# Nesting a width-wise two-output trick into two of six positions of a row-wise fast convolution, in a residual block

## The chip, the cores and the metric

The kernel runs on one core of one Trainium2 chip. The metric is the device time of one execution in microseconds (us).

Engines: PE is TensorE (PEld its weight loads), DVE is VectorE, ACT is ScalarE, POOL is GpSimd, SP issues most DMAs. "L565" is line 565 of the kernel that the line of the profile belongs to.

## The reference

```python
# B, C, H, W = 2, 512, 64, 64; everything in bfloat16
h = conv3(silu(gn(x, g1, be1)), w1)          # gn: group norm, 4 groups of 128 channels
h = h + (silu(t_emb) @ w_emb).reshape(B, C, 1, 1)   # t_emb: 2 x 1152
h = conv3(silu(gn(h, g2, be2)), w2)          # conv3: 3x3, zero padding, C to C channels
return x + h
```

## The kernel before

Both convolutions use a fast algorithm along the rows. Four output rows come from six "positions": the input rows are combined into six tensors V, the weights into six tensors U, each position is a convolution along the width only, and the six results are combined into four rows. A **set** is one block of 128 output channels for one chunk of 32 rows. It is 6 positions x 4 input blocks (of 128 channels) x 3 taps along the width = 72 matmuls of 512 columns. There are 4 output blocks x 4 chunks (2 images x 2) x 2 layers = 32 sets: 1 to 16 are layer 1, 17 to 32 layer 2, four sets to a chunk.

The six accumulators of a set (in PSUM) are evacuated four by ScalarE and two by VectorE:

```python
    stage = ctx.enter_context(tc.tile_pool(name="stage", bufs=4))     # weights as they arrive
    ps_acc = ctx.enter_context(tc.tile_pool(name="ps_acc", bufs=6, space=PSUM))
    POS_ORDER = (1, 2, 3, 4, 0, 5)
    ...
                def mm(pos, ct, kx, first, last):
                    nc.tensor.matmul(                                                 # L565
                        accs[pos][:], lhsT=U[ct][:, SLOT[pos], kx, :], rhs=V[:, ct, SLOT[pos], :, kx:kx + W],
                        start=first, stop=last)
    ...
                def evac(pos):
                    if pos in (1, 2, 3, 4):
                        ...
                        i_a = nc.scalar.activation(out=msl[:, SLOT[pos]], in_=accs[pos][:], ...)   # L579
                    if pos == 4:
                        nc.vector.tensor_tensor(out=sts[:, 0:2], in0=msl[:, 0:2], in1=msl[:, 2:4], op=ALU.subtract)
                        ... # seven more, and in layer 2 three that add x (the residual)
                    elif pos in (0, 5):
                        nc.vector.scalar_tensor_tensor(out=y4[:, (0, 3)[k]], in0=accs[pos][:], ...)   # L599
                    if pos == 5:
                        ... # layer 1: square for the second norm, store to h_scr; layer 2: store to out
```

Everything else (weights' preparation `prep_U`, the input tensors `produce_V`, the statistics of the norms, the embedding) is cut into small steps that a scheduler mixes into the sets ahead of a deadline. In the traces each engine takes its instructions in the order of the program.

Of the kernel before, what the change touches and what calls it, by code (L numbers as in the profile page):

```python
# [64 lines left out]
def kernel(  # L65
# [33 lines left out]
    N_SUM_ACT = 1  # L99
    assert C % P == 0 and E % P == 0 and C // 4 == P and H % CR == 0 and NFREE == 512  # L100
# [8 lines left out]
    stage = ctx.enter_context(tc.tile_pool(name="stage", bufs=4))  # L109
    wtmp = ctx.enter_context(tc.tile_pool(name="wtmp", bufs=2))  # L110
    vpool = ctx.enter_context(tc.tile_pool(name="V", bufs=2))
    srcp = ctx.enter_context(tc.tile_pool(name="src", bufs=2))
    otmp = ctx.enter_context(tc.tile_pool(name="otmp", bufs=1))
    stg = ctx.enter_context(tc.tile_pool(name="stg", bufs=2))
    small = ctx.enter_context(tc.tile_pool(name="small", bufs=4))
# [21 lines left out]
    k_tmp = [consts.tile([P, 2, TR, TH, WP], F16, name=f"k_tmp{i}") for i in range(2)]  # L137
    x_tmp = consts.tile([P, TR, 2, WP], F16, name="x_tmp")
    sum_w = consts.tile([P, NCH, 5], F32, name="sum_w")
    for i, wgt in enumerate((1.0, 1.0, 2.0, 6.0, 2.0)):  # L140
        nc.vector.memset(sum_w[:, :, i:i + 1], wgt)
# [52 lines left out]
    def gram_pe(pieces, pool, tag):  # L194
        gr = pool.tile([P, NFREE], F32, tag=tag, name="gr")
        grf = gr[:, 0:P]
        blocks = [pc[:, j * P:(j + 1) * P] for pc in pieces for j in range(pc.shape[1] // P)]
        for j, blk in enumerate(blocks):
            nc.tensor.matmul(grf, lhsT=blk, rhs=blk, start=(j == 0), stop=(j == len(blocks) - 1))
        return grf  # L200

    def colsum_pe(pieces, pool, tag):
        cs = pool.tile([P, NFREE], F32, tag=tag, name="cs")
        blocks = [pc[:, k * NFREE:(k + 1) * NFREE] for pc in pieces for k in range(pc.shape[1] // NFREE)]
        for k, blk in enumerate(blocks):
            nc.tensor.matmul(cs[:], lhsT=ones_bf[:], rhs=blk, start=(k == 0), stop=(k == len(blocks) - 1))
# [26 lines left out]
    def me_colsum(me_col, cs):  # L233
        junk0 = wtmp.tile([P, NFREE], BF16, tag="sc")
        nc.scalar.activation(out=junk0[:], in_=cs[:], func=ACT.Identity,
# [4 lines left out]
    def gn1_stats_bg(b, ct, dep=None):  # L240
        hp = HW // 2
        pieces = []
        for k in range(2):
            xt = stg.tile([P, hp], BF16, tag="xr")
# [46 lines left out]
    def prep_U(layer, ot, ct, eng=None, dep=None):  # L291
# [3 lines left out]
        U = upool.tile([P, NPOS, NKX, P], F16, tag="U")  # L295
        Ut[layer][ot][ct] = U
# [14 lines left out]
        sc = wtmp.tile([P, 2, NKX, P], F16, tag="scp")  # L311
        nc.vector.tensor_scalar(out=sc[:, 0], in0=g0, scalar1=0.25, scalar2=None, op0=ALU.mult)
        nc.vector.tensor_scalar(out=gg[:, 0], in0=gg[:, 1], scalar1=0.5, scalar2=None, op0=ALU.mult)
        nc.vector.tensor_tensor(out=sc[:, 1], in0=g0, in1=g2, op=ALU.add)  # L314
        nc.vector.tensor_tensor(out=sc[:, 0], in0=sc[:, 0], in1=g2, op=ALU.add)  # L315
        yield
        nc.vector.tensor_tensor(out=U[:, 0:2], in0=sc[:], in1=gg[:], op=ALU.add)  # L317
        nc.vector.tensor_tensor(out=U[:, 2:4], in0=sc[:], in1=gg[:], op=ALU.subtract)  # L318
        yield

# [28 lines left out]
    POS_ORDER = (1, 2, 3, 4, 0, 5)  # L349
    SLOT = {3: 0, 1: 1, 4: 2, 2: 3, 0: 4, 5: 5}  # L350
    Vt = {}
    V_STEPS = 3 * CT

    def produce_V(layer, b, ch, resident=None, V=None):
        if V is None:
            V = vpool.tile([P, CT, NPOS, TR, WP], F16, tag="V")
        Vt[(layer, b, ch)] = V
        r0 = ch * CR - 1
        lo, hi = max(r0, 0), min(r0 + CR + 2, H)
        for ct in range(CT):  # L360
            at = a_tmp[ct % 2]
            if ch == 0:
                nc.gpsimd.memset(at[:, 0, 1:W + 1], 0.0)
            if ch == NCH - 1:
                nc.gpsimd.memset(at[:, CR + 1, 1:W + 1], 0.0)
            if resident is None:
                src = srcp.tile([P, CR + 2, W], BF16 if layer == 0 else F16, tag="src")
                src_dram = x_v[b, ct] if layer == 0 else h_scr[b, ct]
                nc.sync.dma_start(
                    out=src[:, lo - r0:hi - r0, :],  # L370
                    in_=src_dram[:, lo * W:hi * W].rearrange("p (r w) -> p r w", w=W),
                )
                srcs = [(lo, hi, src[:, lo - r0:hi - r0, :])]
            else:
                srcs = []
                for (rs, re, ap3) in resident[ct]:
                    a_, b_ = max(lo, rs), min(hi, re)
                    if a_ < b_:
                        srcs.append((a_, b_, ap3[:, a_ - rs:b_ - rs, :]))
            for (a_, b_, ap) in srcs:  # L380
                nc.scalar.activation(  # L381
                    out=at[:, a_ - r0:b_ - r0, 1:W + 1], in_=ap,
                    func=ACT.Silu, bias=nb_all[:, layer, b, ct:ct + 1],
                    scale=sc_all[:, layer, b, ct:ct + 1],
                )
            kt = k_tmp[ct % 2]

            def rows2(j):
                return at[:, j:j + CR, :].rearrange("p (t f) w -> p t (f w)", f=TH)[:, :, 0:2 * WP]

            nc.scalar.activation(out=kt[:, 1, :, 1:3].rearrange("p t f w -> p t (f w)"), in_=rows2(1),  # L391
                                 func=ACT.Copy, scale=4.0)
            yield
            nc.vector.tensor_tensor(  # L394
                out=kt[:, 0].rearrange("p t f w -> p (t f w)"),
# [42 lines left out]
    for ct in range(CT):  # L438
# [15 lines left out]
        if ct == 0:  # L454
            for g in gens_U0[1:]:
                next(g)
# [209 lines left out]
```

## Time and profile before

| | before |
|---|---|
| time, median of 15 runs | 564.81 us (563.0 to 565.33) |
| profiled span, clock | 563.3 us, 0.995 |
| PE / DVE / ACT busy | 543.4 / 372.5 / 278.2 us |
| an undisturbed set (72 matmuls) | 15.70 us |
| first matmul of set 1; end of the last matmul | 27.3 us; 558.5 us |

From the page of the kernel before: the busy times (first line), then the rows of the busy tenths in 40 equal slices of 14 us.

```profile
PE 543.4 (96%) x2814; PEld 260.8 (46%) x2814; DVE 372.5 (66%) x983; ACT 278.2 (49%) x380; POOL 22.5 (4%) x74
...
PE   5889999999999999999999989999999999999996
...
DVE  2889997489848732994659989399445942223444
ACT  5779999978825732565437348145212211111110
...
PEclk9999999999999999999999999999999999999999
```

TensorE is the limit nearly everywhere. VectorE and ScalarE are nearly full for several slices near the start, and VectorE again in slices 17 and 18 and from 22 to 25. The groups of instructions of the kernel before (line, engine, operation, output and inputs, shapes, count, then busy us, mean ns of one, idle time before it and what ended it):

```profile
L565 PE MATMUL acc<-V,U 128*128 128x512 f16 x2304 | 511.8, 382 | 0.9 <-DVE V L405 0.6
...
L579 ACT ACTIVATE msl<-acc 128x512 f16<-128x512 f32 x128 | 75.8, 593 | 176.2 <-PE acc L565 174.6
...
L599 DVE SCALAR_TENSOR_TENSOR yst<-acc,tt 128x512 f16<-128x512 f32 (+1 forms) x64 | 42.3, 681 | 3.6 <-PE acc L565 3.6
```

A matmul's own 382 ns is its pipelined length; what counts is the distance from one start to the next, which the trace shows as 216 ns in the median (mostly 215 to 223, 218 on average). 72 x 218 ns = 15.70 us a set. TensorE waited only 0.9 us in all in front of these 2304 matmuls.

### The profile page before, as it was taken

How to read it: one execution, taken by the hardware profiler on the slowest of the kernel's cores; microseconds unless marked ns; L12 is line 12 of the kernel's file. 1: busy time of each engine (PE TensorE's matmuls, PEld its weight loads, DVE VectorE, ACT ScalarE, POOL GpSimd, SP SyncE). 2: the span in 40 equal slices, each digit the busy share in tenths (PEclk: the TensorE clock that was granted, in tenths of full speed). 3: DMA queues.
4: the chain of work that ended last, by engine and by line, in shares of the span. 5: the costliest groups of instructions: out<-in, count | busy, mean ns of one | idle time of the engine just before them, and what ended most of it. 6: DMA issues, size and time to landing. Idle time of an engine off the chain costs nothing.

```text
span 563.3 us, 7506 instructions
## 1 busy us (share of the span) xinstructions
PE 543.4 (96%) x2814; PEld 260.8 (46%) x2814; DVE 372.5 (66%) x983; ACT 278.2 (49%) x380; POOL 22.5 (4%) x74
## 2 busy tenths in 40 slices
PE   5889999999999999999999989999999999999996
PEld 4645544444444444444455545444444444444442
DVE  2889997489848732994659989399445942223444
ACT  5779999978825732565437348145212211111110
POOL 1110000111002000000000020000000000000000
PEclk9999999999999999999999999999999999999999
DMA  8517453445701320033223324324221022222200
GB/s 334 211 40 247 157 165 134 143 153 137 261 11 68 106 86 37 39 114 110 70 80 104 135 67 146 113 76 151 76 74 54 24 74 75 76 74 76 74 38 37
DMA packets 18752, 59.81 MB, mean 106 GB/s; under 512 B 2075, under 2 KB 3227, under 8 KB 18331
## 3 DMA queue, kind: packets, MB, share of 16 engines
q1 hardware_dynamic: 18656, 59.32, 31.7%
q8 instruction: 22, 0.36, 0.3%
q14 instruction: 15, 0.12, 0.1%
q10 hardware_dynamic: 59, 0.01, 0.0%
HBM read 42.54 MB, written 16.78 MB: 105 GB/s over the span
## 4 chain that ended last, share of the span: by engine, by line
PE 67%; DVE 22%; ACT 5%; DMA 2%; issue 1%; POOL 1%; DVEq 0%; SPq 0%; ACTq 0%
PE acc L565 65%; DVE U L317 2%; DVE U L318 2%; DVE k_tmp L394 2%; ACT xt L216 2%; DVE yst L599 1%; ACT xt L212 1%; DVE V L408 1%; DVE V L406 1%; DVE V L405 1%; DVE sc L315 1%; DVE sc L314 1%; DVE k_tmp L399 1%; DMA xbuf<-in_x_dram 1%; ACT msl L579 1%
## 5 line engine op out<-in xcount | busy, mean ns | idle before, releaser
L565 PE MATMUL acc<-V,U 128*128 128x512 f16 x2304 | 511.8, 382 | 0.9 <-DVE V L405 0.6
L565 PEld LDWEIGHTS <-U 128*128 128x128 f16 x2304 | 224.3, 98 | 269.5 <-issue 3.3
L579 ACT ACTIVATE msl<-acc 128x512 f16<-128x512 f32 x128 | 75.8, 593 | 176.2 <-PE acc L565 174.6
L584 DVE TENSOR_TENSOR sts<-msl 128x1024 f16<-128x1024 f16 x32 | 22.0, 688 | 138.5 <-ACT msl L579 138.4
L381 ACT ACTIVATE a_tmp<-src,nb_all,sc_all 128x2112 f16<-128x2112 f16 (+1 forms) x28 | 60.2, 2154 | 23.8 <-DVE nb_all L279 5.9
L606 ACT ACTIVATE junk<-yst 128x2048 f16<-128x2048 f16 x16 | 30.6, 1910 | 33.4 <-DVE yst L599 33.2
L599 DVE SCALAR_TENSOR_TENSOR yst<-acc,tt 128x512 f16<-128x512 f32 (+1 forms) x64 | 42.3, 681 | 3.6 <-PE acc L565 3.6
L391 ACT ACTIVATE k_tmp<-a_tmp 128x1056 f16<-128x1056 f16 x32 | 34.7, 1086 | 16.1 <-DVE V L406 15.9
L394 DVE TENSOR_TENSOR k_tmp<-a_tmp 128x2112 f16<-128x2112 f16 x32 | 40.0, 1249 | 2.5 <-ACT a_tmp L381 2.4
L306 ACT ACTIVATE U<-pa 128x768 f16<-128x768 bf16 x32 | 26.3, 821 | 16.5 <-PE pa L302 16.2
L399 DVE TENSOR_TENSOR k_tmp<-k_tmp,a_tmp 128x1056 f16<-128x1056 f16 x32 | 22.4, 700 | 0.0
L405 DVE TENSOR_TENSOR V<-k_tmp 128x1056 f16<-128x1056 f16 x32 | 22.4, 699 | 0.0
L406 DVE TENSOR_TENSOR V<-k_tmp 128x1056 f16<-128x1056 f16 x32 | 22.4, 699 | 0.0
L408 DVE TENSOR_TENSOR V<-k_tmp,x_tmp 128x1056 f16<-128x1056 f16 x32 | 22.4, 699 | 0.0
L585 DVE TENSOR_TENSOR sts<-msl 128x1024 f16<-128x1024 f16 x32 | 21.8, 683 | 0.0
L302 PEld LDWEIGHTS <-wn 128*128 128x128 bf16 x192 | 16.9, 144 | 10.1 <-issue 5.2
L302 PE MATMUL pa<-ident,wn 128*128 128x128 bf16 x192 | 17.4, 229 | 4.0 <-DVE tot L165 2.8
L317 DVE TENSOR_TENSOR U<-sc,gg 128x768 f16<-128x768 f16 x32 | 17.5, 548 | 0.3
L318 DVE TENSOR_TENSOR U<-sc,gg 128x768 f16<-128x768 f16 x32 | 17.5, 546 | 0.0
L308 ACT ACTIVATE gg<-pb 128x384 f16<-128x384 bf16 x32 | 16.1, 503 | 0.1
L216 ACT ACTIVATE xt<-xt 128x2048 bf16<-128x2048 bf16 x8 | 15.3, 1918 | 0.0
L212 ACT ACTIVATE xt<-xt 128x2048 bf16<-128x2048 bf16 x8 | 15.3, 1918 | 0.0
(83 smaller groups left out, 308.7 us busy)
## 6 DMA issues: line engine op xcount, KB each, us to landing
wn<-in_w_dram SPq DMA_DIRECT2D x32, 288.0 KB, 3.3
src<-h_scr SPq DMA_DIRECT2D x16, 528.0 KB, 3.8
h_scr<-yst SPq DMA_DIRECT2D x16, 512.0 KB, 2.9
xr<-in_x_dram SPq DMA_DIRECT2D x16, 512.0 KB, 4.1
out_dram<-yst SPq DMA_DIRECT2D x16, 512.0 KB, 3.7
src<-in_x_dram SPq DMA_DIRECT2D x12, 528.0 KB, 3.9
xt<-in_x_dram SPq DMA_DIRECT2D x8, 512.0 KB, 4.9
xbuf<-in_x_dram SPq DMA_DIRECT2D x3, 1024.0 KB, 6.3
```

Of the source, the lines that this page charges most:

```text
L302: nc.tensor.transpose(pa[:, j, kx, :], wn_v[:, 2 * j, kx, :], ident[:])
L317: nc.vector.tensor_tensor(out=U[:, 0:2], in0=sc[:], in1=gg[:], op=ALU.add)
L318: nc.vector.tensor_tensor(out=U[:, 2:4], in0=sc[:], in1=gg[:], op=ALU.subtract)
L381: nc.scalar.activation(out=at[:, a_ - r0:b_ - r0, 1:W + 1], in_=ap, func=ACT.Silu, bias=nb_all[:, layer, b, ct:ct + 1], scale=sc_all[:, la ...
L391: nc.scalar.activation(out=kt[:, 1, :, 1:3].rearrange("p t f w -> p t (f w)"), in_=rows2(1), func=ACT.Copy, scale=4.0)
L394: nc.vector.tensor_tensor(out=kt[:, 0].rearrange("p t f w -> p (t f w)"), in0=at[:, 2:CR + 2].rearrange("p r w -> p (r w)"), in1=at[:, 0:C ...
L399: nc.vector.tensor_tensor(out=pq, in0=pq, in1=rows2(3), op=ALU.subtract)
L405: nc.vector.tensor_tensor(out=Vc[:, 0:2], in0=rp, in1=sq, op=ALU.add)
L565: nc.tensor.matmul(accs[pos][:], lhsT=U[ct][:, SLOT[pos], kx, :], rhs=V[:, ct, SLOT[pos], :, kx:kx + W], start=first, stop=last)
L579: i_a = nc.scalar.activation(out=msl[:, SLOT[pos]], in_=accs[pos][:], func=ACT.Copy if not kw else ACT.Identity, scale=KAPPA, **kw)
L599: nc.vector.scalar_tensor_tensor(out=y4[:, (0, 3)[k]], in0=accs[pos][:], scalar=(0.25 / WS, 1.0 / WS)[k], in1=tt[:, k], op0=ALU.mult, op1= ...
L606: nc.scalar.activation(out=junk[:], in_=yf, func=ACT.Square, scale=float(HW) ** -0.5, accum_out=ssq[:, ch:ch + 1])
```

## The change

The intent is to do less on the engine that is the limit. Take two neighbouring output columns of one position, with inputs d0..d3 and taps U0, U1, U2:

```
even = U0 d0 + U1 d1 + U2 d2  =  U0 d0 + U1 (d1 + d2)  -  (U1 - U2) d2
odd  = U0 d1 + U1 d2 + U2 d3  =  U0 d1 + U2 (d2 + d3)  +  (U1 - U2) d2
```

The last product is shared. If the sums S = d + (d shifted by one) and Ud = U1 - U2 are at hand, one block costs one matmul of 512 columns and three of 256, 1280 columns in place of 1536. The change does this for two of the six positions (3 and 4), in 28 of the 32 sets (not in the first chunk of layer 1). The matmuls then read every second column. The core of the diff:

```diff
-        accs[pos][:], lhsT=U[ct][:, SLOT[pos], kx, :], rhs=V[:, ct, SLOT[pos], :, kx:kx + W], ...
+    if pos not in nsl:            # plain positions: as before                         (L597)
+    ...
+    S = Vc[:, NPOS + i]
+    nc.tensor.matmul(acc[:], lhsT=Uc[:, s_, 0], rhs=Vc[:, s_, :, 0:W].rearrange("p t (j h) -> p h t j", h=2), ...)   # L604
+    nc.tensor.matmul(acc[:, 0:NH]..., lhsT=Uc[:, s_, 1], rhs=S[:, :, 1:W:2], ...)              # L606
+    nc.tensor.matmul(acc[:, NH:2 * NH]..., lhsT=Uc[:, s_, 2], rhs=S[:, :, 2:W + 1:2], ...)     # L608
+    nc.tensor.matmul(accs["w"][:, i * NH:(i + 1) * NH], lhsT=Ud[:, i], rhs=Vc[:, s_, :, 2:W + 1:2], ...)  # L610
```

The rest makes room for it or follows from it (cuts are marked by "..."):

```diff
# evictions: all six positions on ScalarE, the nested ones written with step two; accumulator w twice
-  nc.vector.scalar_tensor_tensor(out=y4[:, (0, 3)[k]], in0=accs[pos][:], ..., in1=tt[:, k], ...)
+  nc.scalar.activation(out=y4[:, 3 * k], in_=accs[pos][:]..., ...)                               # L617
+  if pos in nsl: dst = dst.rearrange("p (n h) -> p h n", h=2)
+  nc.scalar.activation(out=dst, in_=accs[pos][:]..., scale=KAPPA, ...)                           # L625
+  for h in range(2):
+      nc.scalar.activation(out=wv[:, h], in_=accs["w"][:], scale=(-KAPPA, KAPPA)[h], ...)        # L632
# VectorE adds w (L638), combines (L639-L646), adds into the outer rows at the end (L658)
# nested sums, one per V tile, and Ud, one per U tile
+  nc.vector.tensor_tensor(out=vf[:, NPOS:NSL, 0:n - 1], in0=vf[:, 0:NEST + 1:2, 0:n - 1],
+                          in1=vf[:, 0:NEST + 1:2, 1:n], op=ALU.add)                              # L425
+  nc.vector.tensor_tensor(out=Ud, in0=U[:, 0:3:2, 1], in1=U[:, 0:3:2, 2], op=ALU.subtract)
# memory: V is one tile per input block (8 slots for 6), one k_tmp, fewer staging buffers
-  stage = tile_pool(name="stage", bufs=4)
+  stage = tile_pool(name="stage", bufs=3)
# residual of layer 2: x is copied to out by DMA early, the results are added to it by DMA (not in the last set)
+  nc.sync.dma_start(out=out_v[b, ct][:, cs_], in_=x_v[b, ct][:, cs_])                            # 16 copies
-  nc.sync.dma_start(out=out_v[b, ot][:, rows], in_=flat(yst))
+  nc.gpsimd.dma_start(out=out_v[b, ot][:, rows], in_=flat(yst), accum_op=ALU.add)
# first loads: with three staging buffers, weights 2 and 3 of set 1 are loaded after all of x
-  for g in gens_U0[1:]: next(g)      # directly after x block 0
+  for g in gens_U0[1:2]: next(g)     # weight 1 only; 2 and 3 come after x blocks 1 to 3
```

## The prediction

> **What bounds the kernel now.** TensorE. The page of the profile has it busy 543.4 of 563.3 us at a granted clock of 0.995; 2304 matmuls of 512 columns make 32 sets (4 output blocks x 4 row chunks x 2 layers) of 72. In the chain of waits twelve in a row take 2.62 us, 218 ns each, so 15.7 us a set. Counting matmuls in windows of the trace, sets 9-14 and 20-31 run at 15.6-15.9 us. The others lose: the start (first conv matmul at 27.3 us), sets 2-3 (19.1, 17.9 us), sets 15-19 (16.7, 17.2, 18.3, 18.7, 22.5 us), where layer 2's weights are prepared. In the windows VectorE and ScalarE are 100% busy at 40-80 us, VectorE at 300-320 us.
>
> **What the change does.** In 28 of 32 sets (not the first chunk of layer 1) two of six positions replace three 512-column matmuls per input block by one of 512 and three of 256. In the trace 32 back-to-back 128-column matmuls with their weight loads took 1.79 us (56 ns each); between 56 and 218 ns I estimate 110 ns for 256 columns. Saved: 2x218-3x110 = 106 ns, x8 = 0.85 us a set, 23.8 us in all. The moving reads step by two elements; the Trainium skill (SBUF — State Buffer, the note on cachelines) says accesses within one 16-byte line keep full bandwidth, which step two does. No run shows it yet.
>
> Per set, durations from the instruction groups less about 0.08 us overlap: ScalarE evacuates all six positions plus the shared accumulator twice, four more evictions of 0.59 us. VectorE drops two of 0.68 us and, in layer 2, the residual adds (1.3 us), which become accumulating DMAs; it gains a 1024-element add (0.6). V costs VectorE 5.2-5.9 us per input block instead of 4.2; its nested sum reads one operand off by one element, without 4-byte alignment, so I take the single rate, 1.2 us (VectorE: DVE Perf Modes, mode 2x_1P). Sums over the instruction order: VectorE 372 to about 391 us, ScalarE 278 to about 345 us.
>
> **How much lands.** Sets 9-16, 20-32: TensorE stays the limit, 0.85 x 21 = 17.8 us gained. Sets 17-19: VectorE's work is 57 us before and after, against 50 us of TensorE; they took 59.5 and gain nothing. Sets 1-8: ScalarE has 69 us for sets 3-6 against TensorE's 63, VectorE 51 instead of 41 us in sets 2-4, and 16 copies of x to the output enter the DMA queue ahead of weights: the 3.4 us due there are lost again. The tail, now eviction, add, store: +0.8 us. ScalarE and VectorE wait for each other twice a set; I allow 2.5 us. 564 - 17.8 + 0.8 + 2.5 = 549.5 us.
>
> **Prediction: 549.5 us, 541 to 560 (8 in 10). Faster by over 2%: 0.62; within 2%: 0.32; slower: 0.06.**
>
> **What would show it.** 256-column matmuls about 110 ns apart; late sets at 14.9 us; ScalarE near 345 us; the nested sum at 1.2 us; sets 17-19 still 18-20 us each; set 8 ending at 163-169 us (166 now); TensorE idle for ScalarE's evictions in sets 3-7.
>
> **What would make it wrong.** Strided reads at half rate (over 100 us lost, late sets 19 us or more); weight loads not hidden behind 256 columns; the copies delaying sets 2-3 by more than a few us; ScalarE late enough to fill the six accumulators; accumulating DMAs that hold output buffers or lengthen the tail.

## More of the kernel before

The embedding, `emb_task`, loads nine weight pieces through the `stage` buffers that the convolution's weights use too, makes a silu on ScalarE and 36 small matmuls:

```python
        nc.scalar.activation(out=s_sb[...], in_=ps_t[:], func=ACT.Silu)          # L329
        yield
        for i in range(EMB_NP):                                                  # 5 loads, of up to two pieces
            wt = stage.tile([P, EMB_PIECE, C], BF16, tag="stage")
            nc.sync.dma_start(out=wt[:, 0:n, :], in_=wemb_v[:, e0:e0 + n, :])
            ps_e = ps_x.tile([P, CT, B], F32, tag="x")
            ... matmul(ps_e, lhsT=wt, rhs=s_sb)                                  # L339
            ... emb_sb += ps_e                                                   # VectorE
            yield
```

## The result and the profile after

| | before | after |
|---|---|---|
| time, median (range), runs | 564.81 (563.0 to 565.33), 15 | 559.17 (557.37 to 560.29), 10 |
| ratio of fast runs, 95% interval | | 0.9903 (0.9889 to 0.9917) |
| profiled span, clock | 563.3 us, 0.995 | 557.2 us, 0.985 |
| an undisturbed set | 15.70 us | 15.13 us |
| first matmul of set 1; end of the last | 27.3; 558.5 us | 29.1; 550.3 us |

A ratio is the mean time of one kernel's fast runs over that of the other's fast runs of the same rounds, so it is not quite the ratio of the medians. The change is a gain of 1%, within the 2% that counts as the same. The time lies inside the predicted range of 541 to 560 us, but the gain is 5.6 us where 14.5 were predicted, and "within 2%" had been given a chance of 0.32.

The page of the kernel after, the same rows:

```profile
PE 530.7 (95%) x3038; PEld 282.1 (51%) x3038; DVE 386.2 (69%) x1025; ACT 355.1 (64%) x531; POOL 36.3 (7%) x89
...
PE   5789999999799999999999989999999999999995
...
DVE  3589999833899895497569999779534972223334
ACT  4458679999767485798669855578435833332332
...
PEclk9989999999799999999999999999999999999999
```

TensorE has 12.7 us less work, of which 6.1 us of span came. The slice from 139 to 153 us (the eleventh) is new: PE and PEclk both fall to 7. The groups that answer to those of before, and the new ones:

```profile
L597 PE MATMUL acc<-V,Uf 128*128 128x512 f16 x1632 | 368.2, 383 | 5.5 <-DVE V L416 5.5
...
L625 ACT ACTIVATE ms<-acc 128x512 f16<-128x512 f32 x128 | 83.8, 660 | 85.5 <-PE acc L608 43.0
...
L604 PE MATMUL acc<-V,Uf 128*128 128x512 f16 x224 | 89.1, 398 | 0.0
...
L617 ACT ACTIVATE yst<-acc 128x512 f16<-128x512 f32 (+1 forms) x64 | 38.6, 603 | 47.4 <-PE acc L597 36.8
...
L632 ACT ACTIVATE yst<-accw 128x512 f16<-128x512 f32 x56 | 37.5, 744 | 0.0
```

ScalarE's plain eviction takes 603 ns, the ones that write with step two 744 ns (L632). The 660 of L625 mixes both kinds: in the trace 72 plain ones took 592 ns and 56 with step two 748. The nested sum and, for comparison, a VectorE instruction of nearly the same size whose operands are all aligned, from the groups of VectorE (the first row of the whole run, the second of 28 to 190 us):

```profile
L425 DVE TENSOR_TENSOR V<-V 128x1054 f16<-128x1054 f16 x28 | 19.7, 704 | 0.1
L416 DVE TENSOR_TENSOR V<-V 128x1056 f16<-128x1056 f16 x13 | 9.1, 699 | 0.0
```

A stretch of a late set of the kernel after, from the timeline (start us, length us, engine, line, operation):

```profile
436.13 0.39 PE L604 MATMUL acc<-V,Uf 128*128 128x512 f16 x1
436.36 0.28 PE L606 MATMUL acc<-V,Uf 128*128 128x256 f16 x1
436.48 0.28 PE L608 MATMUL acc<-V,Uf 128*128 128x256 f16 x1
436.59 0.28 PE L610 MATMUL accw<-V,Uf 128*128 128x256 f16 x1
436.71 0.39 PE L604 MATMUL acc<-V,Uf 128*128 128x512 f16 x1
```

From 436.13 to 436.71 one nested block takes 0.58 us. Over sets 25 to 32 the median distances to the next start are 233, 116, 116 and 118 ns, 583 together, where three plain matmuls take 3 x 218 = 654.

**Where the time went, by sets.** The table is worked out from the starts of the convolution's matmuls in the two traces (us; a set's length is the distance to the next set's start).

```
                      before    after    gain
start of set 1         27.35    29.09   -1.74
set 1                  20.07    22.80   -2.73
sets 2-6 (sum)         87.51    83.06   +4.45
set 7                  16.32    22.23   -5.91
set 8                  15.70    15.13   +0.57
sets 9-16 (sum)       129.41   124.96   +4.44
sets 17-19 (sum)       57.90    56.24   +1.65
sets 20-32 (sum)      204.26   196.81   +7.45
after the last matmul   4.78     6.86   -2.08
span                  563.29   557.18   +6.12
```

Three places give back what the sets gain: the start with set 1 (4.5 us), set 7 (5.9 us) and the tail (2.1 us). Set 7 is where the embedding's small products stand in TensorE's queue. From the timeline of TensorE, set 7 before:

```profile
134.50 0.56 PE L339 MATMUL ps_e<-s_sb,wt 128*128 128x2 bf16 x16 [1.02 <-ACT s_sb L329]
134.93 2.78 PE L565 MATMUL acc<-V,U 128*128 128x512 f16 x12
```

and after:

```profile
146.08 0.56 PE L355 MATMUL ps_e<-s_sb,wt 128*128 128x2 bf16 x16 [3.28 <-ACT s_sb L345]
...
148.42 0.63 PE L604 MATMUL acc<-V,Uf 128*128 128x512 f16 x1
148.84 0.41 PE L606 MATMUL acc<-V,Uf 128*128 128x256 f16 x1
149.06 0.41 PE L608 MATMUL acc<-V,Uf 128*128 128x256 f16 x1
149.27 0.41 PE L610 MATMUL accw<-V,Uf 128*128 128x256 f16 x1
149.48 0.63 PE L604 MATMUL acc<-V,Uf 128*128 128x512 f16 x1
...
151.62 1.48 PE L597 MATMUL acc<-V,Uf 128*128 128x512 f16 x6
```

A wait of 1.02 us for the silu became one of 3.28 us, and for the next five microseconds the matmuls of 256 and 512 columns stand 213 and 426 ns apart, twice the usual distance of a plain matmul. The Trainium skill (TensorE: Matmul & The Clock Gate, Part 1) says that TensorE's clock is halved after an idle window of about 3.4 us and gives 426.7 ns for 512 columns at half clock, 215.7 at full. The trace agrees with the two distances, 426 and 216 ns, and the half clock here follows a wait of 3.28 us. (In the kernel before, plain matmuls at half clock, from 336 to 339 us, stand 425 to 428 ns apart, no less than the strided ones here: the extra cost of strided reads, described below, does not show at half clock.) So the set pays twice: 3.3 us of waiting, and half of about 5.1 us at half clock, some 2.6 us more.

The tail, from the timeline: before,

```profile
557.71 0.68 DVE L595 TENSOR_TENSOR yst<-qs,xr 128x1024 bf16<-128x1024 f16 x1
558.31 1.28 DVE L599 SCALAR_TENSOR_TENSOR yst<-acc,tt 128x512 bf16<-128x512 f32 x2
559.62 0.33 SPq L610 DMA_DIRECT2D out_dram<-yst  x1
```

and after:

```profile
550.36 0.60 ACT L617 ACTIVATE yst<-acc 128x512 bf16<-128x512 f32 x1 [2.01 <-PE acc L597]
...
551.27 0.68 DVE L649 TENSOR_TENSOR yst<-yst,xr 128x1024 bf16<-128x1024 bf16 x1
551.88 0.68 DVE L648 TENSOR_TENSOR ms<-ms,xr 128x1024 f16<-128x1024 f16 x1
552.66 0.69 DVE L658 TENSOR_TENSOR yst<-yst,ms 128x1024 bf16<-128x1024 bf16 x1
553.38 0.34 SPq L665 DMA_DIRECT2D out_dram<-yst  x1
```

The last eviction is done at 550.96, but VectorE is still combining the nested positions until 552.6, and the final add starts 1.7 us after the eviction. Before, VectorE took the last accumulator itself and added in the same instruction.

### The profile page after: what moved, and what is told of

Read it like the earlier page. It is cut to its first block, busy times and chain, and to the rows that moved or that the text cites. A ratio compares the mean times of both kernels' runs of the same rounds, so it can differ in the third digit from the quotient of the medians.

```text
span 557.2 us, 8149 instructions
## 1 busy us (share of the span) xinstructions
PE 530.7 (95%) x3038; PEld 282.1 (51%) x3038; DVE 386.2 (69%) x1025; ACT 355.1 (64%) x531; POOL 36.3 (7%) x89
## 4 chain that ended last, share of the span: by engine, by line
PE 65%; DVE 24%; ACT 6%; DMA 2%; POOL 1%; issue 1%; SPq 0%; DVEq 0%; ACTq 0%
PE acc L597 43%; PE acc L604 8%; PE acc L606 4%; PE acc L608 4%; PE accw L610 4%; DVE Uf L323 2%; DVE Uf L322 2%; DVE V L416 1%; DVE V L412 1%; DVE V L411 1%; ACT xt L221 1%; DMA wn<-in_w_dram 1%; DVE k_tmp L413 1%; DVE V L417 1%; PE gr L204 1%; ACT xt L217 1%
## 5 line engine op out<-in xcount | busy, mean ns | idle before, releaser
L597 PE MATMUL acc<-V,Uf 128*128 128x512 f16 x1632 | 368.2, 383 | 5.5 <-DVE V L416 5.5
L597 PEld LDWEIGHTS <-Uf 128*128 128x128 f16 x1632 | 159.6, 99 | 191.7 <-issue 9.7
L625 ACT ACTIVATE ms<-acc 128x512 f16<-128x512 f32 x128 | 83.8, 660 | 85.5 <-PE acc L608 43.0
L604 PE MATMUL acc<-V,Uf 128*128 128x512 f16 x224 | 89.1, 398 | 0.0
L617 ACT ACTIVATE yst<-acc 128x512 f16<-128x512 f32 (+1 forms) x64 | 38.6, 603 | 47.4 <-PE acc L597 36.8
L610 PE MATMUL accw<-V,Uf 128*128 128x256 f16 x224 | 63.0, 281 | 0.0
L608 PE MATMUL acc<-V,Uf 128*128 128x256 f16 x224 | 62.8, 280 | 0.0
L606 PE MATMUL acc<-V,Uf 128*128 128x256 f16 x224 | 62.7, 280 | 0.0
L660 ACT ACTIVATE ms<-yst 128x2048 f16<-128x2048 f16 x16 | 30.6, 1911 | 18.8 <-DVE yst L658 18.8
L632 ACT ACTIVATE yst<-accw 128x512 f16<-128x512 f32 x56 | 37.5, 744 | 0.0
L608 PEld LDWEIGHTS <-Uf 128*128 128x128 f16 x224 | 21.6, 96 | 30.8 <-issue 0.9
L312 ACT ACTIVATE Uf<-pa 128x768 f16<-128x768 bf16 x32 | 26.1, 817 | 7.0 <-PE pa L308 6.9
L604 PEld LDWEIGHTS <-Uf 128*128 128x128 f16 x224 | 22.0, 98 | 7.1
L606 PEld LDWEIGHTS <-Uf 128*128 128x128 f16 x224 | 21.7, 97 | 7.1
L610 PEld LDWEIGHTS <-Uf 128*128 128x128 f16 x224 | 21.6, 97 | 4.8
L639 DVE TENSOR_TENSOR ms<-ms 128x1024 f16<-128x1024 f16 x32 | 22.0, 687 | 0.6
L640 DVE TENSOR_TENSOR ms<-ms 128x1024 f16<-128x1024 f16 x32 | 22.0, 687 | 0.5
```

The source lines that it names most:

```text
L312: nc.scalar.activation(out=U[:, 4:6], in_=pa[:], func=ACT.Copy, scale=WS)
L597: nc.tensor.matmul(acc[:], lhsT=Uc[:, s_, kx], rhs=Vc[:, s_, :, kx:kx + W], start=first and kx == 0, stop=last and kx == NKX - 1)
L604: nc.tensor.matmul(acc[:], lhsT=Uc[:, s_, 0], rhs=Vc[:, s_, :, 0:W].rearrange("p t (j h) -> p h t j", h=2), start=first, stop=False, skip_ ...
L606: nc.tensor.matmul(acc[:, 0:NH].rearrange("p (t j) -> p t j", j=WH), lhsT=Uc[:, s_, 1], rhs=S[:, :, 1:W:2], start=False, stop=False, skip_ ...
L608: nc.tensor.matmul(acc[:, NH:2 * NH].rearrange("p (t j) -> p t j", j=WH), lhsT=Uc[:, s_, 2], rhs=S[:, :, 2:W + 1:2], start=False, stop=las ...
L610: nc.tensor.matmul(accs["w"][:, i * NH:(i + 1) * NH], lhsT=Ud[:, i], rhs=Vc[:, s_, :, 2:W + 1:2], start=first and i == 0, stop=last, skip_ ...
```

## The experiments

Eighteen kernels were run, all of them edits of the changed kernel. Three questions: what the nested matmuls really cost and why; what costs the start, set 7, sets 17 to 19 and the tail; whether a version beats both kernels by more than the change does. Numbers for sets come from the traces as above. Thirteen runs were timed in rounds against the kernel before; `reads`, `nostats`, `defer`, `deint` and `psumstride` are single looks, whose times tell little under 1%, so there only the trace is used.

### reads: which property of the reads costs

The operands are replaced so that results are wrong, with the shapes and counts kept. In layer 1 the matmul of 512 columns and one of 256 read short contiguous runs, the third one run of 256 at step two; in layer 2 they read long contiguous runs, and the third 4 runs of 64 at step two. The shared matmul L610 (L621 here) is unchanged: 8 runs of 32 at step two.

```diff
 # layer 1
+matmul(acc, Uc[0], rhs=T[:, :, 0:W].rearrange("p t (h j) -> p h t j", h=2))   # 16 runs of 32, step 1
+matmul(lo,  Uc[1], rhs=S[:, :, 0:WH])                                          # 8 runs of 32, step 1
+matmul(hi,  Uc[2], rhs=Sflat[:, 0:NFREE:2])                                    # 1 run of 256, step 2
 # layer 2
+matmul(acc, Uc[0], rhs=T[:, :, 0:W])                                           # 8 runs of 64, step 1
+matmul(lo,  Uc[1], rhs=Sflat[:, 0:NH])                                         # 1 run of 256, step 1
+matmul(hi,  Uc[2], rhs=...[:, :, 0:2 * W:2])                                   # 4 runs of 64, step 2
```

> Changes only the access patterns of the four nested matmuls (result wrong on purpose). In the changed kernel the next matmul starts 232 ns after the 512-column one (16 runs of 32 elements at step two) and 116-117 ns after each of 256 columns (8 runs of 32 at step two), where 216 and about 109 were due. In layer 1: the 512 one as 16 runs of 32 at step one, the first 256 one as 8 runs of 32 at step one, the second 256 one as a single run of 256 at step two, the fourth unchanged. In layer 2: the 512 one as 8 plain runs of 64, the first 256 one as one run of 256 at step one, the second 256 one as 4 runs of 64 at step two. Theory STEP (the step of two costs 7%): step-one patterns 216 and 109, step-two patterns 116-117 whatever their runs. Rival RUN (about 1 ns for each short run): 16 runs of 32 at step one still 232, 8 runs still 116, the single run at step two 109-110. Rival WEIGHT (the four weight loads per 1280 columns cost it): nothing changes, 232 and 116 everywhere.

Measured, median distance from start to start (ns):

```
read pattern                         512 columns   256 columns
runs of 64 (512) or 256, step one          215         108.5
runs of 32, step one                       224         113
one run of 256, step two                    -          113
4 runs of 64, step two                      -          117
8 (16) runs of 32, step two                233 (after) 116-118
```

Layer 2 from the timeline of this run, the contiguous reads (the first three distances are 0.22, 0.11 and 0.11 us, the last 256-column pair at step two 0.11 and 0.12):

```profile
435.63 0.38 PE L615 MATMUL acc<-V,Uf 128*128 128x512 f16 x1
435.85 0.27 PE L617 MATMUL acc<-V,Uf 128*128 128x256 f16 x1
435.96 0.28 PE L619 MATMUL acc<-V,Uf 128*128 128x256 f16 x1
436.07 0.28 PE L621 MATMUL accw<-V,Uf 128*128 128x256 f16 x1
```

Neither theory alone holds. Step two costs some nanoseconds and so do short runs, and both were in the change. That weight loads might not be hidden behind 256 columns is excluded: with the same number of weight loads the contiguous matmul takes 108.5 ns. That agrees with the Trainium skill (TensorE: Matmul & The Clock Gate, "Back-to-back issue gap"), which gives 262 cycles for 256 columns, by estimate 109 ns at its 2.4 GHz.

### deint: sums stored so that they are read contiguously

In two of each layer's four chunks VectorE writes the nested sums de-interleaved, evens then odds, with four shorter instructions, so that L606 and L608 read one run of 256.

```diff
+for i in range(NEST):
+    for h in range(2):
+        nc.vector.tensor_tensor(out=vf[:, NPOS + i, h * NH:(h + 1) * NH]...,
+                                in0=V[:, 2 * i, :, 1 + h:W + h:2], in1=V[:, 2 * i, :, 2 + h:W + 1 + h:2], op=ALU.add)
-rhs=S[:, :, 1:W:2]
+rhs=Sf[:, 0:NH] if idx >= 2 else S[:, :, 1:W:2]
```

> In sets 9-16 and 25-32 the nested sums are stored with the odd and the even columns in two blocks, so that two of the three 256-column matmuls read one run at step one; the third and the 512-column one stay strided. Run reads showed 108.5 ns for such a read against 116-117. If that carries over, these two lines show 108-109 ns in those sets and the sets take 15.13 - 16 x 0.008 = 15.0 us, 2 us less in all. VectorE pays for it: four operations of 256 elements that read at step two instead of one of 1054 elements (0.70 us)[...], with VectorE at 50-70% there; if that hurts, sets 8 or 12 grow.

The two matmuls went from 116 to 108 ns in sets 9 to 16 and 25 to 32, those sets from 15.13 to 15.00 us. This is the same effect as in `reads`, in a correct kernel; VectorE's four pieces took 418 ns each in place of one of 704, and no set grew for it.

### psumstride: strided accumulator

The other way round: the matmul of 512 columns reads its moving data in order, and the two of 256 columns, which still read at step two, also write the accumulator at step two.

```diff
-matmul(acc[:], Uc[0], rhs=V...rearrange("p t (j h) -> p h t j", h=2))
+matmul(acc[:], Uc[0], rhs=V[:, s_, :, 0:W])
-matmul(acc[:, 0:NH], Uc[1], rhs=S[:, :, 1:W:2])
+matmul(acc[...even columns...], Uc[1], rhs=S[:, :, 1:W:2])      # and the odd ones for Uc[2]
-dst = dst.rearrange("p (n h) -> p h n", h=2)                    # eviction: now contiguous
```

> The nested positions keep their columns in natural order: the 512-column matmul reads 8 plain runs of 64 (216 ns by run reads instead of 232), but the two of 256 columns write every second fp32 word of the accumulator, and ScalarE evicts without a strided write (0.60 us instead of 0.74). If strided accumulator writes are free, those stay at 116-117 ns and a set takes 15.0 us. If they are costly, as the Trainium skill's page SBUF — State Buffer says in its note on cachelines, the two lines take clearly longer, 130 ns or more, and a set takes 15.2 us or more.

The matmul of 512 columns fell to 215 ns, as in `reads`. The two that write every second accumulator element took 179 and 215 ns in place of 116, and the shared one after them 154; a set is 16.58 us and the run 590.39 us. The Trainium skill (PSUM — Partial Sum Buffer, its table's row on cachelines) says that any non-contiguous pattern there slows matmuls significantly; this run agrees and gives the size for step two. The evictions of the nested positions, now without step two, took 595 ns, and those of w, still written at step two, 744: for these evictions it is the step of the write that costs.

### plain: everything but the nesting

```diff
-nsl = () if (layer == 0 and idx == 0) else NESTED
+nsl = ()            # and no nested sums, no Ud
```

> No set is nested, no nested sums, no weight differences; all other parts of the change stay (new V production, evictions on ScalarE, copies of x and accumulating DMAs, three weight buffers). If the rest of the change is neutral, it takes the time of the kernel before. Sum of what the trace shows lost outside the matmuls: 4.5 us at the start, up to 6 us in set 7, 1 us or less in the tail (no correction): 564 + 5 to 11 = 569 to 575 us. If most of set 7's stall came from the nested sets' two further evictions on ScalarE, set 7 stalls less and it is 567 to 570. Late sets 15.7 us.

574.86 us, ratio 1.0186 (1.0148 to 1.0224) to the kernel before. Undisturbed sets are 15.70 us again. So the nesting by itself is worth 574.86 - 559.17 = 15.7 us, which fits 28 sets x 0.575 us = 16.1; and what the change brings along costs about 10 us. Here, too, set 1 is longer (22.79 us), and sets 6, 9 and 18 lose (20.53, 17.57, 23.83 us).

### order4: the first loads as before, four staging buffers

```diff
-stage = tile_pool(name="stage", bufs=3)
+stage = tile_pool(name="stage", bufs=4)
-for g in gens_U0[1:2]: next(g)
+for g in gens_U0[1:]: next(g)       # all four weights directly after x block 0
```

> Four weight buffers instead of three, and the four first weight blocks are loaded before the rest of x, as in the kernel before. Theory for the start (the changed kernel loads weight blocks 3 and 4 behind x, so that VectorE prepares them at 22-26 us in the middle of the first V instead of in idle time before): the first conv matmul starts at 27.0-27.8 us instead of 29.1, set 2 starts 2-3 us earlier than 51.9. The rest of the start (set 1: 22.8 against 20.1 us) is VectorE's longer V production and stays. Theory for set 18 (the last weight block of layer 2 is issued at 338.8 us, when a third buffer is freed, 323.4 before): with four buffers set 18 takes 17.5-18.5 us instead of 21.0. Together 4 to 6 us less. Rival for the start (the copies of x to the output in the queue): no change before set 2. Rival for set 18 (VectorE 100% busy): no change there.

Set 1 starts at 27.3 us and set 2 at 49.0, 2.9 us earlier than in the changed kernel; the time is 556.98 us (ratio 0.9873, 0.9845 to 0.9901). Two things differ in this run, the order and the fourth buffer. `best6` below moves only one weight forward, with three buffers, and begins set 2 at 49.4 us where `best5`, otherwise the same, begins it at 52.0: so it is the later weights of the first set that the start lost, though `best6` loses the gain again in set 2 (23.05 us). The size is uncertain, as traces whose first loads are those of the change begin set 2 anywhere from 50.2 to 52.6 us, and this run's interval overlaps that of the change (0.9889 to 0.9917). About 1.7 us of set 1's loss stays (21.72 us against 20.07). Sets 18 and 19 stayed at 21.17 and 17.48 us, so they do not lose for want of a fourth staging buffer; that expectation fell. From 296 to 354 us VectorE is busy 56.0 of 58 us after and 55.8 before, by the view of windows: it is nearly full there, as predicted. That it alone sets the length of these sets is not shown: in `plain` it is busy only 51.8 of the 59.8 us that sets 17 to 19 take.

### tail: nested positions first in each set

```diff
-POS_ORDER = (1, 2, 3, 4, 0, 5)
+POS_ORDER = (3, 4, 1, 2, 0, 5)      # w is added after position 4, the rest combined after position 2
```

> The two nested positions come first in every set and their correction is added while the next two positions run; same work. In the changed kernel 6.9 us pass from the end of the last matmul to the end (4.7 before), as the combining chain of VectorE from the end of position 4 (544.9 us) to the store (553.4) takes 8.5 us. Theory (chain from the last of the four positions): the shared accumulator's two evictions and the correction, 2 us, leave the chain; the tail is 4.9-5.2 us, the span falls by 1.6 to 2.2 us, late sets stay at 15.1. Rival (the tail is set by the store or by accumulating DMAs still running): no change of the tail.

Last matmul to end of span: 5.2 us, from 6.9. 558.07 us, ratio 0.9894 (0.9868 to 0.9921), an interval that overlaps that of the change; the trace alone shows the gain. The end of this run's chain, from the timeline of VectorE: the final add starts 0.36 us after VectorE fell idle, at the end of the last eviction, and no longer waits behind other work.

```profile
549.43 0.69 DVE L650 TENSOR_TENSOR ms<-ms,xr 128x1024 f16<-128x1024 f16 x1
550.47 0.69 DVE L660 TENSOR_TENSOR yst<-yst,ms 128x1024 bf16<-128x1024 bf16 x1 [0.36 <-ACT yst L617]
```

### defer: are the copies of x to blame?

The 16 copies of x into the output, which the scheduler issues from 22 to 63 us, are made to wait until set 8 is evacuated.

```diff
+after(nc.sync.dma_start(out=out_v[b, ct][:, cs_], in_=x_v[b, ct][:, cs_]), dep)   # dep: an eviction of set 8
```

> The 16 copies of x to the output, issued at 22-63 us, may only start after set 8. The prediction counted on them to delay the weights of sets 2-3. If they do, sets 1-3 get shorter by 1 us or more in sum (22.8, 19.9, 16.8 now). If VectorE alone bounds sets 1-3, they stay within 0.3 us each, and nothing else changes, as the DMA engines are at 30-60% where the copies now fall.

Sets 1 to 3 took 22.82, 19.88 and 16.79 us, unchanged (22.80, 19.90, 16.79). The copies delay nothing there. Issued later, they cost 2.2 us, in set 11 (17.35 us), where TensorE waited for evictions.

### emb, nostats, emblate, embfirst: set 7

Four runs ask what set 7 waits for. `emb` makes the embedding's silu before the main loop; `nostats` takes away ScalarE's passes for the second image's statistics (wrong, though the result stayed within the tolerance); `emblate` moves the whole embedding into sets 9 and 10; `embfirst` does it all before set 1.

```diff
 # emb
+gen_emb = emb_task(); next(gen_emb)            # the silu, ahead of the main loop
 # nostats
-sum_act(pieces[0:1], part[:, 0:1]); sq_act(pieces[0:1], part[:, 2:3])
+nc.vector.memset(part[:], 0.001)               # the second half's two passes go too
 # emblate
-t_emb_task = bg.add(emb_task(), EMB_STEPS, slot_of(0, 1, CT - 1))
+if b == 0: bg.add(emb_task(), EMB_STEPS, slot_of(0, 2, 1))      # after set 8
 # embfirst
+for _ in emb_task(): pass                      # ahead of the main loop
```

> The silu of t_emb is computed before the main loop instead of in set 7; nothing else. In the changed kernel TensorE waited 3.3 us for it in set 7, its clock fell to 0.74, and the set took 22.2 us instead of 15.1 due. Theory A (ScalarE was only 5 us late, and one small operation in its queue held up TensorE): set 7 takes 15.3-16.5 us, the span falls by 5 to 6.5 us. Rival B (ScalarE has too much to do in sets 3-7, and the wait only moves to the six accumulators): set 7 or 8 still loses 3 us or more, the span falls by less than 3 us.

> The statistics of image 1 are replaced by constants (result wrong on purpose): ScalarE loses 16 operations of 1.92 us and their 16 sums, 34 us, which it runs in sets 3-7; the loads, the small matmuls and the t_emb task stay. Run emb fell: with the silu out of the way set 7 still took 21.4 us, with TensorE waiting for VectorE to read a small result of the statistics, then for loads of w_emb. Theory LATE SCALAR (ScalarE, with its added evictions, finishes the statistics late, at 133 us, so that the small matmuls of statistics and embedding, their VectorE steps and the w_emb loads all fall into the same microseconds and TensorE's queue waits through them): set 7 takes 15.1-16.5 us. Rival EMBEDDING (the chain of the embedding itself, two buffers for the small results and loads that are issued late, costs it wherever ScalarE stands): set 7 still 18 us or more.

> The whole embedding task is moved from sets 5-7 to sets 9-10 where no engine is short. Both theories of set 7 let it fall: under EMBEDDING set 7 takes 15.1-16 us and nothing is lost later, 5.5 to 7 us less in all; under LATE SCALAR the statistics alone can still hold TensorE for some 2 us (as in run plain, 1.9 us in set 6), set 7 takes 16-18 us, and 3 to 5 us are gained. If the chain of the embedding is bad anywhere, sets 9-11 lose 3 us or more instead.

> The whole embedding task (loads, silu, 36 small matmuls, 5 additions) is done before the main loop, while TensorE waits for VectorE's first V anyway. Run nostats showed that ScalarE's statistics are not what stretches set 7, run emblate that the loss goes with the task (set 9 took 21.9, set 10 17.7 us). If the loss is the task's small matmuls standing in TensorE's queue while its inputs are late, then out of a full-rate set it costs nothing: set 7 takes 15.1-16 us, sets 9-10 15.1-15.8 us. Its 1.2 MB of loads now stand ahead of the last weight blocks (3.4 us of DMA time at most), and its small matmuls stand inside set 1, so set 2 may start up to 2 us later. In sum 4.5 to 7 us less than the changed kernel, 552 to 554.5 us.

```
           set 1   set 7   set 9   set 10   start of set 10   time us (ratio to before)
before     20.07   16.32   16.25   15.70        183.2         564.81
after      22.80   22.23   15.77   15.12        188.1         559.17 (0.9903)
emb        21.99   21.38   15.68   15.12        185.5         558.04 (0.9894, 0.9865-0.9923)
nostats    22.82   22.78   15.68   15.12        187.8         558.43 (one look)
emblate    22.80   15.26   21.94   17.70        186.9         561.37 (0.9950, 0.9926-0.9975)
embfirst   27.99   15.26   18.32   15.13        190.5         561.14 (0.9939, 0.9915-0.9963)
```

"The silu is late because ScalarE is busy" fell as the whole cause: with the silu early, `emb`, set 7 still took 21.38 us, now with waits of 1.5 us for a weight and 1.6 us for VectorE. No single wait of its matmuls was longer than 1.6 us, and still the clock stood at half from 146 to 148 us (0.50 by the view of windows). "The statistics keep ScalarE busy" fell too: in `nostats` ScalarE was busy only 35.0 of 63 us from 72 to 135 us, and the wait for the silu even grew, from 3.28 us to 4.84. From the view of waits of `nostats` (in us: total, times, longest):

```profile
PE ps_e L352 <- ACT s_sb L342: 4.8, 1, 4.8
```

In its timeline the silu stands in ScalarE's queue behind the square of the set before (1.91 us), which had itself waited 1.62 us for VectorE's last addition to that set. `emblate` shows that the loss goes where the embedding goes, and in `embfirst` it moves to the start.

### embacc, embpre: the embedding's inputs early

`embacc` makes the silu early and collects all 36 products in one accumulator, which takes VectorE out. `embpre` has in addition six of the nine weight pieces in a buffer of their own.

```diff
 # embacc
-start=(j == 0), stop=(j == n - 1)
+start=(e0 + j == 0 and ot == 0), stop=(e0 + j == ET - 1)       # one accumulator, one copy at the end
 # embpre, in addition
+wtA = consts.tile([P, 6, C], BF16, name="wtA")
+nc.sync.dma_start(out=wtA[:], in_=wemb_v[:, 0:6, :])           # issued at 21.6 us; the last 3 by staging
```

> The silu of t_emb is done before the main loop (as in run emb), and the 36 small matmuls of the embedding now add up in one accumulator that VectorE reads once, instead of five, each read by VectorE before the second next can start. The loads stay: two of the five wait for a free weight buffer. Theory ROUND TRIPS (set 7 is stretched because TensorE's queue meets, in the embedding, one wait after another on ScalarE, on VectorE's reads of the two small buffers and on loads): set 7 takes 15.1-17.5 us, the span falls by 5 to 7 us against the changed kernel. If the loads behind the buffers are the larger part: set 7 takes 18-20 us. If something else in these microseconds stretches set 7: 21 us or more, as in run emb.

> The changed kernel with the embedding's inputs ready early: its silu is made before the main loop, six of the nine weight pieces of the embedding are loaded into a buffer of their own that nothing else uses, the last three into two staging buffers, and all 36 products go into one accumulator. WAIT-FOR-INPUTS theory (set 7 loses 5.9 us over the set of the kernel before, 22.2 against 16.3, because the tensor engine waits over 3 us for one input of the embedding, a silu or a weight behind other loads in the queue, and then runs at half clock): set 7 takes 15.2 to 16.5 us, no other set of 1 to 16 grows by more than 2 us, and the span falls by 4 to 7 us, to about 551. If instead the embedding's 36 small products cost time of their own wherever they stand, some set of 2 to 10 is longer by 4 us or more and the span stays within 2 us of 557.

`embacc`: set 7 took 20.76 us; what is left is a wait of about 3 us for a weight of the embedding, whose load stands behind other loads in the one queue, and half clock after it. 557.55 us, ratio 0.9875 (0.9857 to 0.9893). 

`embpre`: set 7 took 16.22 us, as expected, so the wait for the embedding's inputs is what made set 7 long. The other half of the expectation fell: set 9 grew from 15.77 to 23.10 us, and the time is 559.17 us (ratio 0.9912, 0.9887 to 0.9937), no gain at all. The timeline of TensorE in set 9 of this run:

```profile
170.11 0.39 PE L611 MATMUL acc<-V,Uf 128*128 128x512 f16 x1
175.55 0.59 PE L169 MATMUL ps<-me,ones_neg 128*128 128x2 f32 x2 [5.05 <-DVE me L280]
176.00 0.38 PE L613 MATMUL acc<-V,Uf 128*128 128x256 f16 x1
...
180.08 0.46 PE L611 MATMUL acc<-V,Uf 128*128 128x512 f16 x1
```

TensorE now arrives 7.7 us earlier at set 9 (164.6 us for 172.3) and waits 5.05 us there for a small matmul of the second norm's statistics, whose operand VectorE had not made; half clock until 180.08 costs another 2 us or so. The view of windows shows how busy VectorE is. The columns are the stretch in us, its length, and busy us (number of instructions) of PE, PEld, DVE, ACT and POOL, then clock, DMA share and GB/s. Before:

```profile
72.00:135.00 63.00, 61.51 (x315) 28.96 (x314) 48.27 (x132) 57.25 (x77) 5.15 (x13) 1.00 0.41 135
135.00:172.00 37.00, 37.00 (x191) 16.89 (x189) 27.10 (x81) 23.57 (x31) 0.46 (x3) 1.00 0.47 152
```

after:

```profile
72.00:135.00 63.00, 63.00 (x329) 31.35 (x328) 44.73 (x130) 60.60 (x94) 3.64 (x10) 1.00 0.36 123
135.00:172.00 37.00, 33.63 (x199) 17.34 (x198) 33.75 (x90) 27.58 (x40) 1.71 (x7) 0.91 0.53 163
```

and `embpre`:

```profile
135.00:172.00 37.00, 35.51 (x220) 18.79 (x218) 36.03 (x96) 27.00 (x41) 1.68 (x7) 1.00 0.43 133
```

From 135 to 172 us VectorE was busy 27.1 of 37 us before; in `embpre` it is busy 36.0 (35.9 in `best5` below), and it is nearly full. In the stretch before, 72 to 135 us, ScalarE is nearly full (57.3, after 60.6 of 63 us), and VectorE does less than before (44.7 against 48.3 us).

### best2, lean, best4, best5, best6: the parts together

```diff
 best2 = tail + embfirst + order4
 lean  = tail + order4 + deint
 best4 = lean + embacc
 best5 = tail + deint + embpre
 best6 = best5, and weight 2 of the first set loaded ahead of x blocks 1 to 3 (three staging buffers)
```

> Embedding before the main loop, four weight buffers with the old order of the first loads, and the nested positions first in every set. If the three losses are separate, their gains add: 5 to 7 (set 7), 2 (start, run order4), 1 to 1.5 (tail, run tail): 8 to 10.5 us less than the changed kernel's 559, that is 549 to 551.5 us. If the embedding's loads, now beside the early weight loads, take back the start's gain, 551 to 553 us.

> Old order of the first loads with four weight buffers, nested positions first, sums stored in two blocks; the embedding untouched. Gains of the single runs, if they add: 2.1 (order4), 0.9 to 1.4 (tail), 2.0 (deint) us: 559 - 5 = 553.5 to 554.5 us.

> As lean, with the embedding of embacc. If ROUND TRIPS holds: 547 to 549.5 us, 2.5 to 3% under the kernel before. If it falls: 552 to 554 us.

> The early embedding of the run beside it, with the nested sums stored in de-interleaved order and the nested positions first in each set. WAIT-FOR-INPUTS theory: the gains add, de-interleaving 2.7 us, tail 1.5 to 2, set 7 about 5; time 548 to 552. If the set-7 loss only moves elsewhere, as it did in the two runs with it at the start or later, 555 or more.

> As the run before, and the third input weight block of the first set is loaded ahead of the rest of x. Set 2 starts 0 to 2.9 us earlier than in the run before it; time 546 to 552 if the gains add; no better than the run before it if the first set is bound by x and its statistics instead.

```
           start of   set 1   set 7   set 9   start of   time us   ratio to before (95%)
           set 1                              set 10
best2       28.3      26.87   15.26   20.76    192.2     561.53    0.9937 (0.9904-0.9969)
lean        27.8      21.72   23.82   15.59    187.7     554.84    0.9831 (0.9806-0.9855)
best4       27.6      21.72   26.17   15.55    189.8     557.42    0.9866 (0.9845-0.9888)
best5       29.1      22.81   16.22   25.18    191.3     558.40    0.9889 (0.9862-0.9916)
best6       27.7      21.71   16.22   25.35    192.3     559.07    0.9911 (0.9886-0.9935)
```

`lean` is the best kernel found, 1.7% faster than the kernel before and some 0.7% faster than the change by the two ratios, 0.9831 and 0.9903. It takes the parts whose gain was seen by itself: 15.00 us sets in half of the chunks, the tail of 5.2 us, the earlier start. Every version that also repairs set 7 loses at set 1, 7 or 9 what it gains. In all of these runs set 10 starts at 185.5 to 192.3 us, before at 183.2: between the start and set 10 most of what one set gains another loses. `psumstride` says the same from the other side: its matmuls are slower, sets 5, 6 and 8 take 16.6 to 16.7 us, but set 7 shrinks to 18.35 us and set 9 starts at 172.0 us, as after the change (172.3).

What stays open is what holds set 10 near 187 us. VectorE's amount of work, or its order behind a full ScalarE, is the obvious guess, but `nostats` speaks against either as the whole cause: with ScalarE busy 35.0 of 63 us, VectorE did 54.9 us of work from 72 to 135 us and was busy only 25.7 of 37 us from 135 to 172, and set 10 still started at 187.8 us, with a wait of 4.84 us for the silu before it. No run takes away that wait and ScalarE's statistics together, so the cause is not shown.

## Why the prediction was right or wrong

**Wrong: the size of the saving per nested block.** The step that failed is the sum "Saved: 2x218-3x110 = 106 ns, x8 = 0.85 us a set, 23.8 us in all", and within it that step two "keeps full bandwidth". The prediction took this from the Trainium skill (SBUF — State Buffer, the note on cachelines), and said that no run showed it. Measured: 654 - 583 = 71 ns a block, 0.575 us a set, 16.1 us in all. The prediction counted on 21 of these 28 sets: its term "0.85 x 21 = 17.8 us gained" came as 11.9, 5.9 us short. That is the largest miss in its sum; the next is sets 1 to 8, 5.4 us lost where no change was forecast. Together they are more than the missing 8.9 us (14.5 predicted, 5.6 measured), because sets 17 to 19 gained 1.7 us and the 2.5 us allowed for waits were not spent. Of the missing 35 ns, the 512-column matmul has 15 (233 for 218) and the three of 256 columns 20 (116 to 118 for the estimated 110). `reads` shows that with long contiguous runs the matmuls would have taken 215 and 108.5 ns, so the estimate of 110 ns was right for contiguous data; step two and short runs are the rest, each shown to cost by itself in `reads`. `deint` recovers part of it. The late sets predicted at 14.9 us came at 15.13.

**Right: TensorE stays the limit in sets 9 to 16 and 20 to 32.** These gained 4.44 + 7.45 = 11.9 us in the profiled runs; the 17.8 predicted, scaled by 0.575/0.85, is 12.0.

**Right in sum by luck, wrong in place: the costs of the rest.** The prediction charged 9.3 us: 6.0 for sets 1 to 8 and 17 to 19 (their share of the 23.8), 0.8 for the tail, 2.5 for waits. `plain` puts the cost at about 10 us. But errors in both directions cancelled. With 0.575 us due in each nested set, the traces give 7.7 us lost in sets 1 to 8 (3.4 charged), 2.1 in the tail (0.8), and only 0.1 in sets 17 to 19 (2.6) and 0.2 of waits in the others (2.5).

- Sets 1 to 8, "the 3.4 us due there are lost again": they lost 5.4 us on balance against the kernel before. The reasons given were ScalarE's 69 us in sets 3 to 6 and the copies. `defer` shows the copies to be innocent. Sets 2 to 6 even gained 4.5 us, and TensorE did not wait for evictions there: from 72 to 135 us it was busy 63.0 of 63 us. What lost is the order of the first loads (`order4`, `best6`), which the prediction did not read from the diff, and a wait of 3.3 us for the embedding's silu with 2.6 us of half clock behind it, which it did not think of at all. The check "set 8 ending at 163-169 us" failed: 172.3.
- Sets 17 to 19, "gain nothing": 57.90 to 56.24 us. VectorE is busy 96 to 97% of that stretch in both kernels, as predicted.
- The tail, "+0.8 us": +2.1. The prediction counted eviction, add and store, and missed that the nested positions stood late in the set's order, so that their combination runs into the tail. `tail` takes 1.7 us of it away.

**The smaller terms.** The nested sum was put at 1.2 us because one operand is off by one element; the Trainium skill (VectorE: DVE Perf Modes, "Mode 2×_1P") asks for 4-byte alignment for the double rate. It took 704 ns, the same as an aligned instruction of the same size (699): here the rule did not bind. VectorE came to 386 us (predicted 391), which is luck: 28 sums at 0.70 us in place of 1.2 are 14 us less, so the rest of its work came out some 9 us longer than predicted. ScalarE came to 355 us (predicted 345). The 112 evictions that write at step two take about 745 ns, not 590, which alone is 17 us more; the prediction's other terms for ScalarE were some 7 us too high in sum.

**What the case teaches about the size of the expectation.** The range held the time, at its edge. The chance of 0.62 for more than 2% rested mostly on one estimate that no trace of the kernel before could test, as it has no matmul that reads at step two. An error of 35 ns a block in it cost 5.9 us of the gain counted on; with these 5.9 us the gain would have been some 11.5 us, just about 2%, and the losses of sets 1 to 8 would still have kept it below 14.5.

## What to carry to other kernels

Before counting saved columns, cost the moving reads by their pattern: a cut from 1536 to 1280 columns a block gave two thirds of its arithmetic worth, and laying the data out contiguously gave part of the rest back. On an engine that is nearly always busy, a wait can cost well over its own length, as the clock is halved after it: here 3.3 us became 5.9, and 5.05 us about 7; look in the queue for small matmuls whose inputs come from another busy engine or from far back in a load queue. And when removing a wait gains nothing, look for what holds the next set: here moving the embedding about mostly moved the loss with it.

## What the Trainium skill lacked or had wrong

- SBUF — State Buffer, the note on cachelines: two hits in a 16-byte line are said to give full bandwidth. With four fp16 elements used of each line (step two), matmuls of 256 columns took 113 to 118 ns against 108.5 contiguous, and the one of 512 in 32-element runs 233 against 215. Part of that is the short runs (next point), and the page's penalty for crossing to a new line has no size. Together they took most of the 35 ns that were missing of every 106.
- No page consulted has the cost of short runs in TensorE's moving reads: at step one, runs of 32 took 113 ns (256 columns) and 224 ns (512), against 108.5 and 215 for long ones.
- PSUM — Partial Sum Buffer, the row on cachelines: right, but without a size. Accumulating at step two took 179 and 215 ns for 256 columns, and the contiguous matmul after them 154 in place of 116.
- VectorE: DVE Perf Modes, "Mode 2×_1P": the page asks for 4-byte alignment. With one operand of an fp16 addition off by one element, 1054 elements (2 x 527) took 704 ns against 699 ns for 1056 aligned ones, so the rate did not depend on it. The skill itself has this right elsewhere (Vector Engine (DVE) Microarchitecture Reference, section 5.1: alignment makes no difference).
- No page consulted has the cost of ScalarE's strided write: an eviction of 512 columns took 744 ns at step two, 595 to 603 ns contiguous.
- TensorE: Matmul & The Clock Gate: its half-clock and full-clock distances (426.7 and 215.7 ns for 512 columns, 262 cycles for 256) are what the runs show (426, 216 and 108.5 ns). In "Back-to-back issue gap" it also gives about 131 ns a matmul as sustained at 512 columns; no stretch here went below 215.
